# Asking for the first three expert-weight pieces one by one, and splitting weight pieces at other places of a tick

## The chip, the cores and the metric

The kernel runs on one core of one Trainium2 chip. The metric is the device time of one execution in microseconds (us). Engines are called as the profile calls them: PE is the matrix engine (PEld its weight loads), DVE the vector engine, ACT the scalar engine, POOL the general engine, SP the engine that here only issues transfers. A row's "PEclk" is the granted share of PE's full clock of 2.4 GHz; 0.50 is its lower level, 1.2 GHz.

## The reference

Two stages. The first is a delta-rule linear attention over 768 steps for 4 x 8 heads of width 48; the second sends each of the 3072 tokens through one of 8 experts, the one with the largest logit.

```python
k_n = k / (np.linalg.norm(k, axis=-1, keepdims=True) + 1e-06)
for t in range(S):
    kt, vt, bt = (k_n[:, :, t], v[:, :, t], beta[:, :, t, None])
    y[:, :, t] = np.einsum('bhd,bhde->bhe', q[:, :, t], state)
    v_old = np.einsum('bhde,bhd->bhe', state, kt)
    state = state + bt[:, :, :, None] * np.einsum('bhd,bhe->bhde', kt, vt - v_old)
...
expert_idx = np.argmax(x @ w_gate, axis=1)
for e in range(E):
    xe = x[expert_idx == e]
    h = np.maximum(xe @ w1[e], 0.0)
    out[expert_idx == e] = gate_w[expert_idx == e, None] * (h @ w2[e])
```

w1 is 8 x 384 x 1024 and w2 is 8 x 1024 x 384, all in 32-bit floats.

## The kernel before

**The attention part** treats 24 blocks of 128 steps (6 time blocks of each of 4 batches), four at a time, each a quarter further along. The loop over `t` from 0 to 26 makes one *tick* of each step. A tick is a chain over three engines: PE makes `ks` from the state and earlier results (`residual`, L423 and L435), DVE subtracts it from `v_all` (L442), PE applies the block's inverse (`apply`, L450), ACT copies the four results into `u` (L454), PE uses them to finish one block (`finish`: `yp` in L473, the state's update `ku` in L482, `yp` again in L491), then `pq` (L265) for a later block, and then the next tick's `ks`. `xp` (L515) turns a finished block into rows of tokens, between `ks` and `apply`. DVE adds `ku` to the state (L486).

**Routing** runs beside the ticks. `emit_slots` takes two finished blocks, finds each token's expert and slot in small DVE steps (L533 to L581, with the matmuls `pp` in L551 and L554 between `oh_all` and `pos`), and POOL scatters the rows into `xg` in DRAM, one scatter (L588) for each block. After the second scatter of one certain pair SP loads 256 rows of expert 0 back as `xr` (`load_main`, L730); `early` (L783) transposes them in tick 23 and starts expert 0 in the ticks after that.

**Expert weights** come in pieces (`pieces`): per expert three pieces of w1, each 128 x 1024 (512 KB), and four of w2, each 128 x 2 x 384 (384 KB). A piece is asked for by `load` (L708, on SP), lands in one of three raw buffers, and is *split*: ACT casts it to the high part (L693), DVE subtracts that from the piece for the low part (L694). `split` serves other tiles with the same two lines too. A split frees the raw buffer, and right behind it the program asks for the piece three further on. The seven pieces that the table `WSL` of pairs (tick, place) takes in ticks 20 to 23 are all of expert 0.

**The order** is written out by hand. `beside(t, i)` is called at seven places i of each tick; place 0 stands right behind `residual` with its subtraction, place 1 ahead of `apply`, places 3 and 4 behind the copies to `u`, place 6 at the tick's end. Each engine, and SP's queue of transfers, does its instructions in that written order: a transfer that has to wait holds every one behind it on SP.

Of the kernel before, what the change touches and what calls it, by code (L numbers as in the profile page):

```python
# [41 lines left out]
def deltanet_moe(ctx, tc, kt_d, qt_d, kn_d, v_d, beta_d, w_gate, w1, w2, out):  # L42
# [102 lines left out]
    TOK0 = (0, 5, 8, 9, 10)  # L145
    PC0 = (0, 2, 5, 7, 8, 10, 11)

    WSL = ((20, 3), (21, 3), (21, 6), (22, 3), (22, 6), (23, 3), (23, 6))
    ES = ((23, 2), (23, 4), (23, 6), (24, 1), (24, 2), (24, 3), (24, 5), (25, 1), (25, 2), (25, 4), (25, 6), (26, 1), (26, 4))
    EF = (4, 8, 9, 10, 12, 13, 14, 15)  # L150
    EO = 'xxxhhhhhhhhytyyo'
# [516 lines left out]
    def run(gen, steps=1):  # L668

        for _ in range(steps):  # L670
            if next(gen, tiles) is tiles:
                return False
        return True
# [18 lines left out]
    def split(hi, lo, src):  # L692
        nc.scalar.copy(out=hi, in_=src)  # L693
        nc.vector.tensor_tensor(out=lo, in0=src, in1=hi.bitcast(F32), op=ALU.subtract)  # L694

    def pieces():

        todo = []
        for e in range(E):
            for nm, src, kk, ff, st in (("w1", w1[e], KD, FF, 1), ("w2", w2[e], KF, DM, 2)):  # L700
                todo += [(e, nm, src.rearrange("(k p) f -> p k f", p=128), kk, ff, st, j) for j in range(0, kk, st)]
        raws = []

        def load(k):
            e, nm, sv, kk, ff, st, j = todo[k]
            raw = wq[0].tile([128, FF], F32, name=f"{nm}r{e}_{j}", tag="wr", bufs=3)
            raws.append(raw[:, 0:st * ff].rearrange("p (k f) -> p k f", k=st))
            nc.sync.dma_start(out=raws[k], in_=sv[:, j:j + st])  # L708

        for k in range(AH):  # L710
            load(k)
        yield
        for k, (e, nm, sv, kk, ff, st, j) in enumerate(todo):
            if j == 0:
                WW[e][nm] = [wq[e % 2].tile([128, kk, ff], F32R, name=f"{nm}{x}{e}", tag=f"{nm}{x}") for x in "hl"]
            hi, lo = WW[e][nm]
            split(hi[:, j:j + st], lo[:, j:j + st], raws[k])
            if k + AH < len(todo):
                load(k + AH)
            yield  # L720
# [254 lines left out]
    def beside(t, i):  # L975
# [8 lines left out]
        for _ in range(STEPS[i] if t < NN - B else 4):  # L984
            if fine and not run(fine[0]):
                fine.pop(0)
        for _ in range(WSL.count((t, i))):
            run(W)
# [4 lines left out]
    for t in range(NN + LAG):  # L993
        if t < NN and t % B == 0 and t > 0:
            while line and line[0].tb <= t // B:
                inverse_step(t)
            if t == NN - B:
                ep_.close()
                wq.append(ep.enter_context(tc.tile_pool(name="wr", bufs=1, side="right")))
                xq_.append(ep.enter_context(tc.tile_pool(name="xq", bufs=1, side="right")))  # L1000
                W = pieces()
                run(W)
# [343 lines left out]
```

## Time and profile before

| what | value |
|---|---|
| median of 3 runs | 526.83 us (522.76 to 527.09) |
| the profiled execution's own time | 525.81 us |
| its span, first to last instruction | 524.1 us |
| PE / DVE / ACT / POOL busy | 461.2 / 339.3 / 268.2 / 143.8 us |
| mean granted clock | 0.947 |

The profiled execution is 1.7 us longer than its span (what lies around the first and last instruction), and 1.0 us under the median. Busy shares are means over a program of two halves: the ticks of the attention part take the first 300 us or so, with all engines in turn; in the experts behind it PE is nearly always busy. Ticks 20 to 23, which the change touches, lie between 223 and 265 us.

### The profile page before, as it was taken

The page shows a single profiled execution, that of the slowest core. Times are in us where ns is not written, and L with a number is a line of the kernel's source. Part 1 is how long each engine was busy: PE and PEld are TensorE (multiplying, and loading weights), DVE is VectorE, ACT ScalarE, POOL GpSimd, SP SyncE. Part 2 cuts the span into 40 slices and gives each one's busy share as a digit, 9 for nine tenths or more (in the row PEclk, how much of TensorE's full clock was granted, in tenths as well). Part 3 has the DMA queues.
Part 4 walks back from the last instruction along what each step waited for, and adds up shares of the span by engine and source line. Part 5 has one row for each costly group of instructions (what it writes and reads, how often), then busy time and mean ns, then how long its engine had stood idle before and what let it go on. Part 6 is the DMA issues. An engine that isn't in the chain of part 4 may idle for free. (4 is left out here: it accounts for less than half of the span.)

```text
span 524.1 us, 17587 instructions
## 1 busy us (share of the span) xinstructions
PE 461.2 (88%) x7212; PEld 424.4 (81%) x7212; DVE 339.3 (65%) x1024; ACT 268.2 (51%) x622; POOL 143.8 (27%) x305
## 2 busy tenths in 40 slices
PE   5764788979988887977889999999999999999995
PEld 3654677767867776866689899999999999999995
DVE  2989999898989988327554386636372737445330
ACT  2442255776866665846634246535364636344320
POOL 7002021465665555442230301020202020110202
PEclk8877789999999988989999989999999999999998
DMA  5887879687578455574442166555373746453001
GB/s 160 191 265 181 277 177 308 180 239 232 115 236 275 141 182 165 174 253 133 142 154 80 63 170 206 178 168 160 120 227 116 209 127 210 142 163 108 33 3 44
DMA packets 66060, 87.88 MB, mean 168 GB/s; under 512 B 26425, under 2 KB 50767, under 8 KB 65968
## 3 DMA queue, kind: packets, MB, share of 16 engines
q1 hardware_dynamic: 62512, 77.01, 50.0%
q0 software_dynamic: 3456, 9.57, 5.0%
q8 instruction: 67, 1.10, 0.9%
q14 instruction: 25, 0.20, 0.1%
HBM read 60.24 MB, written 23.56 MB: 160 GB/s over the span
## 5 line engine op out<-in xcount | busy, mean ns | idle before, releaser
L769 PE MATMUL y<-w2h,hx 128*128 128x384 f32 x352 | 93.9, 341 | 0.4 <-PEq L1142 0.4
L772 POOL DMA_INDIRECT out_dram<-yo,idx x32 | 30.7, 958 | 202.0 <-ACT yo L1115 129.5
L694 DVE TENSOR_TENSOR w2l<-w2r,w2h 128x768 fp32r<-128x768 f32 x32 | 31.2, 978 | 69.8 <-ACT w2h L693 69.7
L383 DVE TENSOR_TENSOR tmp<-lg,lw 128x99 f32<-128x99 f32 (+29 forms) x253 | 69.1, 308 | 3.0
L387 DVE TENSOR_TENSOR lw<-lw,tmp 128x99 f32<-128x99 f32 (+29 forms) x253 | 68.6, 306 | 0.4
L454 ACT COPY u<-ks 32x384 f32<-32x384 f32 x96 | 45.0, 469 | 44.3 <-PE ks L450 41.4
L769 PEld LDWEIGHTS y<-w2h,hx 128*128 128x128 f32 x352 | 64.1, 188 | 0.7 <-issue 0.7
L769 PE MATMUL y<-w2l,hx 128*128 128x384 f32 x176 | 59.4, 337 | 0.0
L758 PE MATMUL h<-xl,w1h 128*128 128x384 f32 (+1 forms) x168 | 57.5, 342 | 0.2 <-DVE xl L694 0.2
L758 PE MATMUL h<-xh,w1h 128*128 128x384 f32 (+1 forms) x168 | 57.5, 342 | 0.0
L758 PE MATMUL h<-xh,w1l 128*128 128x384 f32 (+1 forms) x168 | 57.4, 342 | 0.0
L450 PE MATMUL ks<-v_all,wt 32*32 32x48 f32 x1536 | 26.8, 209 | 29.5 <-DVE v_all L442 25.1
L450 PEld LDWEIGHTS ks<-v_all,wt 32*32 32x32 f32 x1536 | 22.3, 110 | 34.3 <-DVE v_all L442 28.2
L761 ACT ACTIVATE hx<-h 128x448 fp32r<-128x448 f32 (+1 forms) x64 | 32.7, 517 | 31.6 <-PE h L758 28.6
L276 POOL TENSOR_SCALAR_AFFINE_SELECT pm<-pm 128x1024 f32<-128x1024 f32 x24 | 26.7, 1112 | 79.8 <-ACT pm L275 72.4
L423 PE MATMUL ks<-st,kt 128*32 128x96 f32 x768 | 46.8, 261 | 1.0 <-issue 1.0
L762 DVE SCALAR_TENSOR_TENSOR hx<-h,hx 128x448 fp32r<-128x448 f32 (+1 forms) x64 | 36.8, 586 | 15.0 <-ACT hx L761 14.9
L1115 ACT ACTIVATE yo<-y,gt 128x384 f32<-128x384 f32 x21 | 12.2, 582 | 66.5 <-PE y L769 50.7
L248 ACT COPY gg<-pg 128x512 f32<-128x512 f32 x48 | 25.8, 588 | 31.0 <-PE pg L265 31.0
L423 PEld LDWEIGHTS ks<-st,kt 128*32 128x32 f32 x768 | 35.1, 116 | 4.7 <-issue 1.8
L265 PE MATMUL pq<-qt,kt 64*128 64x128 f32 x384 | 31.7, 296 | 4.0 <-issue 2.8
L265 PEld LDWEIGHTS pq<-qt,kt 64*128 64x128 f32 x384 | 26.3, 197 | 9.1 <-issue 4.4
(194 smaller groups left out, 988.2 us busy)
## 6 DMA issues: line engine op xcount, KB each, us to landing
w1r<-in_w_dram SPq DMA_DIRECT2D x24, 512.0 KB
w2r<-in_w_dram SPq DMA_DIRECT2D x32, 384.0 KB
kt<-in_kt_dram SPq DMA_DIRECT2D x24, 256.0 KB
qt<-in_qt_dram SPq DMA_DIRECT2D x24, 256.0 KB
xg<-zrow SPq DMA_DIRECT2D x7, 788.0 KB
kg<-in_kt_dram SPq DMA_DIRECT2D x17, 256.0 KB
xr<-xg SPq DMA_DIRECT2D x7, 591.0 KB
xn<-row SPq DMA_DIRECT2D x10, 394.0 KB
```

The source lines that it names most:

```text
L265: nc.tensor.matmul(pg[a][:, p], lhsT=kt[r, p], rhs=xt[r, p], start=True, stop=True, tile_position=(64 * a, 0), skip_group_check=True)
L383: nc.vector.tensor_tensor(out=x, in0=lg[:, r0:r1, c:c + 1].broadcast_to([128, r1 - r0, b - a]), in1=lw[:, c:c + 1, a:b].broadcast_to([128, ...
L387: nc.vector.tensor_tensor(out=lw[:, r0:r1, a:b], in0=lw[:, r0:r1, a:b], in1=x, op=ALU.add)
L423: nc.tensor.matmul(ks[32 * q:32 * q + 32, 2 * p:2 * p + 2, :], lhsT=kt_t[n % KTL][:, p, 32 * q:32 * q + 32], rhs=st_view(n % B, p), start= ...
L450: nc.tensor.matmul(ks[r, h, :], lhsT=tiles[n // B]["wt"][r, n % B * H + h, :], rhs=vn[r, h, :], start=True, stop=True, tile_position=(32 * ...
L454: nc.scalar.copy(out=uview(n)[r], in_=ks[r])
L694: nc.vector.tensor_tensor(out=lo, in0=src, in1=hi.bitcast(F32), op=ALU.subtract)
L758: nc.tensor.matmul(ps, lhsT=w[:, d, fs], rhs=x_[:, d], start=(n == 0), stop=(n == len(terms) - 1))
L761: nc.scalar.activation(out=hh, in_=ps, func=AF.Relu)
L762: nc.vector.scalar_tensor_tensor(out=hl, in0=ps, scalar=0.0, in1=hh.bitcast(F32), op0=ALU.max, op1=ALU.subtract)
L769: nc.tensor.matmul(ps, lhsT=h(f)[h_], rhs=w2[w][:, f, :], start=(n == 0), stop=(n == len(terms) - 1))
L772: nc.gpsimd.indirect_dma_start(out=out, out_offset=bass.IndirectOffsetOnAxis(ap=idx, axis=0), in_=yo, in_offset=None, bounds_check=N - 1, ...
```

## The change

In `pieces` the `yield` moves into the loop over the first three loads, so that each call asks for one piece. The first stays where it was, at the start of tick 20; the second and third are asked for at places 2 and 5 of that tick. The table then holds nine pairs in place of seven: two for these loads and seven for the same seven splits, which move from (20,3), (21,3), (21,6), (22,3), (22,6), (23,3), (23,6) to (21,1), (21,3), (22,1), (22,3), (23,0), (23,1), (23,3).

```diff
-    WSL = ((20, 3), (21, 3), (21, 6), (22, 3), (22, 6), (23, 3), (23, 6))
+    WSL = ((20, 2), (20, 5), (21, 1), (21, 3), (22, 1), (22, 3), (23, 0), (23, 1), (23, 3))
...
         for k in range(AH):
             load(k)
-        yield
+            yield
         for k, (e, nm, sv, kk, ff, st, j) in enumerate(todo):
```

No instruction is added or taken away. How the order moves is shown at three places, before first and then after.

SP's queue from the first weight piece on, at the start of tick 20 (`w1r_0` to `w1r_2` are expert 0's w1 pieces, `w2r_0` its first w2 piece, `u` a fill with zeros, `xn` a write of token rows, `ku` and `qt` loads for later ticks):

```order
L708 DMA w1r_0_4492<-in_w_dram 128x1024
L708 DMA w1r_1_4494<-in_w_dram 128x1024
L708 DMA w1r_2_4496<-in_w_dram 128x1024
L412 DMA u_4569<-zrow 96x384
L661 DMA xn<-row_2_4203 128x2x394
L200 DMA ku_4633<-in_kn_dram 128x384
L708 DMA w2r_0_4643<-in_w_dram 128x2x384
L195 DMA qt_117<-in_qt_dram 128x512
L412 DMA u_4720<-zrow 96x384
```

```order
L708 DMA w1r_0_4492<-in_w_dram 128x1024
L412 DMA u_4565<-zrow 96x384
L661 DMA xn<-row_2_4203 128x2x394
L708 DMA w1r_1_4618<-in_w_dram 128x1024
L200 DMA ku_4631<-in_kn_dram 128x384
L708 DMA w1r_2_4648<-in_w_dram 128x1024
L195 DMA qt_117<-in_qt_dram 128x512
L412 DMA u_4714<-zrow 96x384
L708 DMA w2r_0_4728<-in_w_dram 128x2x384
```

The second piece now stands behind the zero fill and the row write, the third behind the load of `ku`, and the first w2 piece behind `qt` and the next fill.

DVE at the end of tick 21 and the start of tick 22 (`sli` is the slot list that the scatters need, `v_all<-v_all,ks` the subtraction of tick 22):

```order
L573 TENSOR_REDUCE sl_all<-pos_0_4797 128x2
L581 CAST sli_0_4830<-sl_all 128x2
L694 TENSOR_TENSOR w1l_4640<-w1r_2_4496,w1h_4639 128x1024
L442 TENSOR_TENSOR v_all<-v_all,ks_4837 128x384
L517 TENSOR_REDUCE rl_2_4883<-xp_2_4884 128x8
L406 TENSOR_TENSOR v_all<-v_all,nt_all 128x384
L486 TENSOR_TENSOR st_137<-st_137,ku_3_4944 48x4x48 x2
```

```order
L573 TENSOR_REDUCE sl_all<-pos_0_4797 128x2
L581 CAST sli_0_4830<-sl_all 128x2
L442 TENSOR_TENSOR v_all<-v_all,ks_4833 128x384
L517 TENSOR_REDUCE rl_2_4879<-xp_2_4880 128x8
L406 TENSOR_TENSOR v_all<-v_all,nt_all 128x384
L694 TENSOR_TENSOR w1l_4725<-w1r_2_4648,w1h_4724 128x1024
L486 TENSOR_TENSOR st_137<-st_137,ku_3_4944 48x4x48 x2
```

The split of the third piece has moved from ahead of the subtraction to behind it.

SP's queue in ticks 22 and 23, from the load of `w2r_4` or what stands ahead of it (`xr` are expert 0's rows, which wait for the scatters; the last row is expert 1's first piece):

```order
L708 DMA w2r_4_4835<-in_w_dram 128x2x384
L412 DMA u_4892<-zrow 96x384
L730 DMA xr_4897<-xg 128x2x394
L708 DMA w2r_6_4960<-in_w_dram 128x2x384
L708 DMA w1r_0_4988<-in_w_dram 128x1024
```

```order
L412 DMA u_4888<-zrow 96x384
L730 DMA xr_4893<-xg 128x2x394
L708 DMA w2r_4_4897<-in_w_dram 128x2x384
L708 DMA w2r_6_4960<-in_w_dram 128x2x384
L708 DMA w1r_0_5030<-in_w_dram 128x1024
```

The piece `w2r_4` was asked for ahead of `xr` and now is behind it.

ACT at the start of tick 23 (`u<-ks` are the copies that PE waits for):

```order
L516 COPY row_2_4882<-xp_3_5032 128x384
L539 COPY row_2_4882<-ids_88 128x2x2
L454 COPY u_4373<-ks_4990 32x384
L454 COPY u_4569<-ks_4990 32x384
L454 COPY u_4720<-ks_4990 32x384
L693 CAST xe<-xt_5096 128x256
L454 COPY u_4892<-ks_4990 32x384
L693 CAST w2h_4956<-w2r_4_4835 128x768
```

```order
L516 COPY row_2_4878<-xp_3_5032 128x384
L539 COPY row_2_4878<-ids_88 128x2x2
L693 CAST w2h_4956<-w2r_4_4897 128x768
L454 COPY u_4373<-ks_4986 32x384
L454 COPY u_4565<-ks_4986 32x384
L454 COPY u_4714<-ks_4986 32x384
L693 CAST xe<-xt_5100 128x256
L454 COPY u_4888<-ks_4986 32x384
```

The cast of `w2r_4` has moved from behind the four copies to ahead of them. On DVE its subtraction now stands ahead of `oh_all` of tick 23, and the first piece's ahead of `oh_all` of tick 21.

## Rows read from the trace of the kernel before

**Rows 1.** The page, DMA queues: packets, MB, share of 16 engines

```profile
q8 instruction: 67, 1.10, 0.9%
```

**Rows 2.** Windows: stretch, length, busy us (count) of each engine, PEclk, DMA share, GB/s

```profile
222.30:227.05 4.75, 4.75 (x130) 3.98 (x129) 1.84 (x5) 3.61 (x9) 3.54 (x11) 1.00 0.93 277
227.05:229.85 2.80, 0.05 (x3) 0.05 (x2) 1.23 (x1) 0.50 (x2) 1.90 (x1) 0.99 1.00 363
229.85:233.65 3.80, 3.80 (x87) 3.43 (x87) 0.00 (x0) 1.07 (x2) 0.00 (x0) 0.56 0.88 280
...
245.60:251.10 5.50, 5.50 (x128) 4.69 (x128) 2.16 (x5) 3.34 (x7) 1.84 (x2) 0.69 0.49 138
...
265.30:300.00 34.70, 33.25 (x427) 30.14 (x427) 14.63 (x72) 12.49 (x31) 5.84 (x6) 1.00 0.25 86
```

**Rows 3.** Timeline of PE, ticks 19 to 24: start, us, what, [idle before <-releaser]

```profile
219.27 1.16 PE L265 MATMUL pq<-qt,kt 64*128 64x128 f32 x16
...
223.18 0.88 PE L450 MATMUL ks<-v_all,wt 32*32 32x48 f32 x64
...
226.12 0.93 PE L265 MATMUL pq<-qt,kt 64*128 64x128 f32 x10
229.81 1.22 PE L265 MATMUL pq<-qt,kt 64*128 64x128 f32 x6 [2.75 <-issue]
...
234.72 0.56 PE L450 MATMUL ks<-v_all,wt 32*32 32x48 f32 x33
236.74 0.54 PE L450 MATMUL ks<-v_all,wt 32*32 32x48 f32 x31 [1.46 <-issue]
...
245.59 0.88 PE L450 MATMUL ks<-v_all,wt 32*32 32x48 f32 x64 [2.05 <-DVE v_all L442]
...
254.92 0.88 PE L450 MATMUL ks<-v_all,wt 32*32 32x48 f32 x64 [1.00 <-DVE v_all L442]
...
257.22 0.17 PE L551 MATMUL pp<-oh_all,ltri 128*128 128x16 bf16 x1 [0.28 <-DVE oh_all L547]
...
265.28 0.88 PE L450 MATMUL ks<-v_all,wt 32*32 32x48 f32 x48 [0.47 <-DVE v_all L442]
```

**Rows 4.** Timeline of DVE at the turn from tick 21 to tick 22

```profile
243.84 1.23 DVE L694 TENSOR_TENSOR w1l<-w1r,w1h 128x1024 fp32r<-128x1024 f32 x1
244.98 0.55 DVE L442 TENSOR_TENSOR v_all<-v_all,ks 128x384 f32<-128x384 f32 x1
...
258.84 0.96 DVE L694 TENSOR_TENSOR w2l<-w2r,w2h 128x768 fp32r<-128x768 f32 x1 [0.67 <-ACT w2h L693]
```

**Rows 5.** Timeline of ACT in ticks 20 to 22

```profile
224.13 1.95 ACT L454 COPY u<-ks 32x384 f32<-32x384 f32 x4 [0.36 <-PE ks L450]
225.98 1.04 ACT L693 CAST w1h<-w1r 128x1024 fp32r<-128x1024 f32 x1
...
252.19 0.85 ACT L693 CAST w2h<-w2r 128x768 fp32r<-128x768 f32 x1
```

**Rows 6.** Timeline of SP: transfers asked for in tick 20, and the load of `xr`

```profile
220.97 1.33 SPq L708 DMA_DIRECT2D w1r<-in_w_dram  x3
222.41 0.52 SPq L412 DMA_DIRECT2D u<-zrow  x1
...
225.36 0.33 SPq L200 DMA_DIRECT2D ku<-in_kn_dram  x1
...
252.83 0.37 SPq L730 DMA_DIRECT2D xr<-xg  x1
```

**Rows 7.** Timeline of POOL: the two scatters ahead of that load

```profile
244.21 1.72 POOL L588 DMA_INDIRECT xg<-row,sli  x1 [1.13 <-DVE sli L581]
249.59 1.52 POOL L588 DMA_INDIRECT xg<-row,sli  x1 [3.66 <-DMA xg<-row,sli]
```

**Rows 8.** Windows right behind that load, columns as in Rows 2

```profile
252.80:253.80 1.00, 1.00 (x9) 0.94 (x8) 0.73 (x1) 0.24 (x1) 0.67 (x1) 1.00 0.08 16
253.80:257.40 3.60, 2.19 (x89) 1.62 (x88) 3.10 (x10) 2.03 (x6) 0.00 (x0) 1.00 0.84 244
```

## The prediction

> **What bounds the kernel now.** I read the page first: PE is busy 88% of the span, but that is a mean over two halves. The windows say where it is not. From 265 to 300 us it is busy 33.25 of 34.70 us [rows 2], so there only less work helps, and this change takes none away; what it can give must come from ticks 20 to 23. PE's timeline shows them [rows 3]. From `pq` at 219.27 to the next `pq` at 226.12 PE waits for nothing, so a tick without a wait takes 6.85 us: 2.94 from `apply` (223.18) to `pq`, 3.91 from `pq` to the next `apply`. Counted from `apply` to `apply`, ticks 20 to 23 take 11.54, 10.87, 9.33 and 10.36 us (starts at 223.18, 234.72, 245.59, 254.92 and 265.28 [rows 3]).
>
> Tick 20: PE stops within `pq` for 2.75 us and "issue" is named: no semaphore, no engine. Behind it the granted clock is 0.56 for 3.8 us, partly the level of 1.2 GHz [rows 2], and from 229.81 to `apply` PE needs 4.91 us where 3.91 - 0.93 = 2.98 would do: 1.93 lost. 6.85 + 2.75 + 1.93 is the 11.5 us. Tick 21: 1.46 us of "issue" in mid-`apply`, then 2.05 us for DVE. Tick 22: 1.00 for DVE, and a clock of 0.69 over 5.5 us [rows 2], which leaves 9.33 - 6.85 - 1.00 = 1.48 for the lower clock. Tick 23 holds early expert work, and 0.47 for DVE.
>
> What is an "issue" pause? The program itself comes by DMA: 67 packets, 1.10 MB, so 16 KB each [rows 1]. From the first pause to the second PE does 6 `pq`, 80 `ks` and 8 `xp` matmuls and 33 of `apply` [rows 3], with the 80 and 8 counted in the code: 127, a regular block. The first comes when three pieces (1,536 KB) were asked for in 1.33 us [rows 6]; DMA then moves 277 GB/s, and 363 in the pause itself, all engines taken [rows 2]. I read it as a page of program that stands in line behind weights. The Trainium skill (Runtime: NRT & Kernel Launch, section Instruction fetch mechanics) says that 16 KiB blocks of 256 instructions are fetched while the one before runs, and that a crossing is mostly hidden; by that the 2.75 us would have another cause, and the loads' spreading would save nothing there. The trace has 2.75 and 1.46 us not hidden, so I go by the trace and keep the other reading as a rival.
>
> **The change part by part.** The same transfers, casts and subtractions are made, so only places count.
>
> *The loads, tick 20.* SP issues in order, and the second piece stands behind a zero fill (144 KB) and a row write (394 KB), neither of which waits long: the fill goes out at 222.41, right behind the pieces [rows 6]. So the place (20,2) in the table does not set its time; it goes out perhaps 1.7 us after the first. The third stands behind `ku`, which goes at 225.36. Ahead of the page then are 512 + 144 + 394 = 1,050 KB, 486 KB fewer, 1.4 to 1.8 us at 363 to 277 GB/s; or 656 KB if the page overtakes the row write, 2.5 to 3.2 us. The pause becomes 0 to 1.35 us; if the second piece gets ahead of the page too, it stays 2.75. I take 0.5, between the first two, since the three pieces went in one run and the page asked for at a fixed point now meets one. After the 1.46 us pause no lower clock cost is seen (236.74 to 245.59 is 8.85, less 2.05 is 6.80, against about 6.35 for what was left of that tick), so the 1.93 goes. Tick 20: 7.35 us, `apply` at 230.5 instead of 234.7.
>
> *What is late next: the page in `apply`.* It stands behind all that was asked for in tick 20. That sum falls by only the first w2 piece (384 KB, 0.39 MB, 1.4 us at 280 GB/s), which now waits for the split at (21,1). So PE goes on not at 236.74 but at 235.3, or 234.6 if one scatter (128 rows, 197 KB, 0.7 us) also falls behind the page; ends 233.5 and 236.0. I take 234.6. PE is there at 230.5 + 0.5 = 231.0 and pauses 3.6 us, over twice as long as before. A pause that long brings back the lower clock: 1.48 to 1.93 us by the two cases above, I take 1.6.
>
> *The splits, tick 21.* The cast at (21,1) (1.04 us) and its subtraction (1.23) fit into that pause, ahead of `oh_all`, and cost nothing; without the pause they would put the copies to `u` and `pp` 0.6 to 1.2 us later. The third piece's subtraction was the last thing on DVE ahead of tick 22's (243.84, 1.23 us, then 244.98 [rows 4]); it leaves, and with the first piece's gone from behind the cast chain the 2.05 us wait goes too (at worst 0.8 stays). `apply` of tick 22: 234.6 + 6.8 + 1.6 = 243.0, 2.6 us earlier than before.
>
> *Tick 22.* No wait for DVE, no lower clock, but the cast at (22,1) is ahead of the copies. They began 0.95 us after `apply` in tick 20 (224.13 [rows 5]); the row copy ends about 0.55 after it, the cast 1.04 later, at 1.6: 0.65 lost. 7.5 us, `apply` of tick 23 at 250.5, 4.4 earlier.
>
> *Tick 23: a new wait.* `w2r_4` is now asked for behind `xr`, and its cast stands ahead of the copies to `u`. `xr` waits for both scatters. Before, the first began at 244.21 and the second 5.4 later, and `xr` went out at 252.83, 3.24 behind the second [rows 6, 7]: 8.6 in all, or 6.5 if the first were as quick as the second; I take 7.2, as less traffic is ahead of the first. The first began 1.4 ahead of an `apply` that was late; I take 0.9 (0.4 to 1.4), so 242.1, and `xr` at 249.3. In the first microsecond behind `xr` almost nothing moved (share 0.08), then 244 GB/s [rows 8]: `xr` and a w2 piece are 0.80 MB, 3.3 us, so the piece is there at 253.6 (4.3 behind; ends 3.9 and 4.5). ACT would cast it 0.75 after `apply` (row copy, a small copy), at 251.25: 2.35 us of waiting, with the copies to `u` behind it on ACT. On DVE `oh_all` stands behind the piece's subtraction, and PE's `pp` behind that: cast 0.85 [rows 5], subtraction 0.96 [rows 4], 0.2 for `oh_all`, so `pp` at 255.6. Before it came 2.30 behind `apply` [rows 3], now that is 252.8: 2.8 us of PE, and 1.5 for the clock behind such a pause, less the 0.47 for DVE. Tick 23: 10.36 + 2.8 + 1.5 - 0.47 = 14.2, and tick 24's `apply` at 264.7 instead of 265.28. Ends: 11.1 if everything is early, 16.7 if late.
>
> *The sum.* 4.2 gained in tick 20, 1.6 given back in 21, 1.8 gained in 22, 3.8 given back in 23: 0.6 us. Behind 265 us PE is the bound and the gain is kept. The profiled execution took 525.81, so **525.2 us**; that execution is 1.0 under the median of 526.83, so a median may lie a microsecond higher.
>
> **The rivals.** *The second page is not late (faster).* If it comes as PE reaches it (231.0), tick 22's `apply` is at 238.5 with the casts' 0.7, tick 23's at 246.0, tick 24's 14.2 later at 260.2: 5.1 less, 520.7. For it: in most ticks no such pause is seen. Against it: in tick 21 one was, behind the same traffic. With `w2r_4` in time as well (11.1) 517.6.
>
> *The pause is not from the loads (no change).* By the rule cited above, the 2.75 stays. Then tick 21's `apply` is at 234.7 as before; its own tick is 6.85 + 0.5 + 1.46 = 8.8, tick 22 7.5, tick 23 14.2: 265.2, and 525.7. Against it: the full DMA engines and the regular block.
>
> *The copies wait longer behind `w2r_4` (slower).* With both scatters as slow as before, tick 23 takes 16.7 us, and tick 24's `apply` is at 267.2: 527.7. It decides from the point at which the piece lands later than about 254.2, 3.7 us behind tick 23's `apply`. For it: the order leaves no other way, and `xr` moves with the ticks, so earlier ticks do not help. Against it: 3.24 us is what a scatter needs with little beside it. Its tail is worse: expert 1's three pieces then follow close on each other, and one more page behind 1,536 KB would cost another 2.75 + 1.93.
>
> **How the numbers follow.** The forecast 0.50; the second page on time 0.22 (0.06 of it with `w2r_4` in time); no effect of the loads 0.10; slower 0.18. The likeliest gives 525.2. The range takes in the faster rival at 520.7 with a microsecond for the unknown first pause, and the slower one with 1.8 for part of its tail: 519.5 to 529.5. A change of 1% is 5.3 us, about what a measurement of this kernel can tell from none (its three runs lie 4.3 apart). Below 520.5 I put 0.18, from the faster rival and early ends; above 531.1 0.10, the slower one's tail; 0.72 between.
>
> **What would show it.** Right: no "issue" pause over 1.4 us in tick 20's `pq`, a longer one in tick 21's `apply` with a low clock behind it, no wait for DVE ahead of tick 22's `apply`, and ACT idle ahead of the cast of `w2r_4` with `xr` asked for shortly before. Wrong: a 2.75 us pause at the same matmul; tick 21 without a pause; or that cast without idle time ahead of it.

## The result and the profile after

The change makes the kernel a little slower: 527.83 us median of 20 runs (523.93 to 533.49), against 525.51 (521.08 to 530.75) of the kernel before measured beside it, ratio 1.0079 with a 95% interval of 1.0050 to 1.0109. Two more measurements (below) gave 1.0047 [1.0006, 1.0087] and 1.0064 [1.0014, 1.0114]. By these ratios 0.5 to 0.8% is lost, 2.5 to 4.2 us; the medians of the three pairs lie 2.3, 1.8 and 2.0 us apart. Ratios and their intervals compare undisturbed runs alone (within 1.5% of their kernel's fastest), medians all runs, and the profiles of e2, e7 and e12 below are of disturbed runs, so no reading rests on them. The forecast was 0.6 us gained; the time itself lies in the stated range.

The profiled execution took 528.31 us, with a span of 526.6 us, 2.5 more than before, and a mean granted clock of 0.939 where it was 0.947. Of the 2.5, 1.42 lie ahead of tick 20 (its `apply` starts at 224.60, before at 223.18). They are there already when the first weight piece goes out (at 222.43, before at 220.97 [rows 6]), and up to that request both programs do the same in the same order; in other profiles that start falls anywhere from 222.4 to 230.3, so it is no effect of the change. From tick 24's `apply` to the end of the span it is 258.8 us in both. The ticks between hold the rest:

| tick | before [rows 3] | forecast | after |
|---|---|---|---|
| 20 | 11.54 | 7.35 | 7.07 |
| 21 | 10.87 | 12.5 | 12.26 |
| 22 | 9.33 | 7.5 | 8.12 |
| 23 | 10.36 | 14.2 | 15.77 |
| sum | 42.10 | 41.55 | 43.22 |

PE's timeline of the changed kernel, with the same columns and lines as [rows 3]:

```profile
224.60 0.88 PE L450 MATMUL ks<-v_all,wt 32*32 32x48 f32 x64
...
227.55 1.48 PE L265 MATMUL pq<-qt,kt 64*128 64x128 f32 x16
...
231.67 0.56 PE L450 MATMUL ks<-v_all,wt 32*32 32x48 f32 x33
234.55 0.86 PE L450 MATMUL ks<-v_all,wt 32*32 32x48 f32 x31 [2.31 <-issue]
...
243.93 0.88 PE L450 MATMUL ks<-v_all,wt 32*32 32x48 f32 x64
...
246.18 0.66 PE L473 MATMUL yp<-qt,st 64*64 64x128 f32 x13 [1.01 <-issue]
...
252.05 0.88 PE L450 MATMUL ks<-v_all,wt 32*32 32x48 f32 x64
...
255.10 0.41 PE L783 MATMUL xt<-ident,xr 128*128 128x128 f32 x2 [1.57 <-DMA xr<-xg]
257.99 0.17 PE L551 MATMUL pp<-oh_all,ltri 128*128 128x16 bf16 x1 [2.48 <-DVE oh_all L547]
...
267.82 0.88 PE L450 MATMUL ks<-v_all,wt 32*32 32x48 f32 x48
```

In tick 20 `pq` is one row of 16 (227.55): the 2.75 us pause is gone. In tick 21 `apply` stops behind its 33rd matmul as before, now for 2.31 us. Tick 22's `apply` (243.93) waits for nothing, but in `yp` behind it (246.18) there is a pause that [rows 3] don't have. In tick 23 PE waits for `xr` and then 2.48 us for `oh_all`. Windows of the same execution, columns as in [rows 2]:

```profile
227.50:231.65 4.15, 4.15 (x107) 3.73 (x104) 0.57 (x2) 1.72 (x5) 1.29 (x2) 1.00 1.02 366
231.65:234.50 2.85, 0.59 (x34) 0.43 (x33) 2.05 (x7) 1.52 (x3) 0.00 (x0) 0.91 0.30 102
234.50:241.20 6.70, 6.65 (x99) 5.61 (x99) 3.63 (x13) 3.57 (x7) 2.08 (x2) 0.53 0.36 102
...
252.00:255.10 3.10, 1.53 (x82) 1.20 (x81) 2.55 (x8) 0.57 (x2) 0.00 (x0) 1.00 1.01 333
255.10:258.00 2.90, 0.42 (x3) 0.25 (x4) 1.04 (x2) 1.90 (x4) 0.00 (x0) 0.98 0.50 200
258.00:264.00 6.00, 6.00 (x46) 4.70 (x48) 2.73 (x10) 3.94 (x10) 0.00 (x0) 0.50 0.62 172
264.00:267.80 3.80, 3.80 (x89) 3.62 (x83) 1.95 (x5) 0.70 (x2) 2.08 (x2) 0.90 0.45 169
267.80:300.00 32.20, 30.63 (x408) 27.80 (x408) 14.23 (x71) 12.29 (x31) 4.86 (x5) 1.00 0.21 71
```

With the loads one by one the DMA engines stay full (share 1.02, 366 GB/s), and the clock at its full level. Behind the pause of tick 21 the granted clock is 0.53 for 6.7 us, behind the wait in tick 23 it is 0.50, the lower level of 1.2 GHz throughout, for 6.0: together over 12 us at or near the lower level, where before it was 0.56 for 3.8 us and 0.69 for 5.5 [rows 2].

ACT and then DVE in tick 23:

```profile
252.53 0.20 ACT L539 COPY row<-ids 128x4 f32<-128x4 f32 x1
256.03 0.83 ACT L693 CAST w2h<-w2r 128x768 fp32r<-128x768 f32 x1 [3.30 <-DMA w2r<-in_w_dram]
256.88 1.46 ACT L454 COPY u<-ks 32x384 f32<-32x384 f32 x3
```

```profile
243.02 0.56 DVE L442 TENSOR_TENSOR v_all<-v_all,ks 128x384 f32<-128x384 f32 x1 [1.87 <-PE ks L435]
...
254.68 0.17 DVE L544 TENSOR_REDUCE m<-oh 128x2 f32<-128x16 f32 x1
256.89 0.96 DVE L694 TENSOR_TENSOR w2l<-w2r,w2h 128x768 fp32r<-128x768 f32 x1 [2.04 <-ACT w2h L693]
257.77 0.17 DVE L547 TENSOR_TENSOR oh_all<-oh,m 128x16 bf16<-128x16 f32 x1
```

ACT stands idle for 3.30 us for a w2 piece, ahead of the copies to `u`; on DVE the piece's subtraction stands ahead of `oh_all`, and PE gets `pp` at 257.99, 5.94 us behind `apply`, where it was 2.30 [rows 3]. The first DVE row is tick 22's subtraction, which now waits for `ks` alone: the third piece's split is behind it. What SP had asked for, and POOL's scatters ahead of it (compare [rows 6, 7]):

```profile
250.24 0.37 SPq L730 DMA_DIRECT2D xr<-xg  x1
250.70 0.93 SPq L708 DMA_DIRECT2D w2r<-in_w_dram  x2
252.59 0.34 SPq L708 DMA_DIRECT2D w1r<-in_w_dram  x1
```

```profile
243.70 0.99 POOL L588 DMA_INDIRECT xg<-row,sli  x1 [0.16 <-DVE v_all L442]
246.58 1.03 POOL L588 DMA_INDIRECT xg<-row,sli  x1 [1.89 <-DMA xg<-row,sli]
```

The second scatter starts 2.88 us behind the first (before 5.4), and `xr` goes out at 250.24, 6.54 us behind the first scatter. `w2r_4` is cast 5.8 us after that. The second w2 piece and expert 1's first w1 piece were asked for right behind it, and share the DMA engines (share 1.01): from 250.20 to the cast some 1.5 MB move (windows of 67, 333 and 413 GB/s), where `xr` and one w2 piece are 0.80.

### The profile page after: what moved, and what is told of

Its sections match the earlier page's. It is cut to its first block, busy times and chain, and to the rows that moved or that the text cites. A ratio compares the mean times of both kernels' runs of the same rounds, so it can differ in the third digit from the quotient of the medians.

```text
span 526.6 us, 17587 instructions
## 1 busy us (share of the span) xinstructions
PE 464.5 (88%) x7212; PEld 427.1 (81%) x7212; DVE 336.1 (64%) x1024; ACT 269.2 (51%) x622; POOL 146.6 (28%) x305
## 5 line engine op out<-in xcount | busy, mean ns | idle before, releaser
L387 DVE TENSOR_TENSOR lw<-lw,tmp 128x99 f32<-128x99 f32 (+29 forms) x253 | 70.6, 314 | 0.4
L383 DVE TENSOR_TENSOR tmp<-lg,lw 128x99 f32<-128x99 f32 (+29 forms) x253 | 67.4, 301 | 3.0
L276 POOL TENSOR_SCALAR_AFFINE_SELECT pm<-pm 128x1024 f32<-128x1024 f32 x24 | 30.7, 1281 | 85.6 <-ACT pm L275 82.9
L450 PE MATMUL ks<-v_all,wt 32*32 32x48 f32 x1536 | 25.6, 206 | 26.2 <-DVE v_all L442 21.4
L265 PE MATMUL pq<-qt,kt 64*128 64x128 f32 x384 | 33.0, 309 | 0.7 <-ACT gg L248 0.7
L769 PEld LDWEIGHTS y<-w2l,hx 128*128 128x128 f32 x176 | 33.2, 188 | 0.0
```

The lines of the kernel that those rows point to most:

```text
L265: nc.tensor.matmul(pg[a][:, p], lhsT=kt[r, p], rhs=xt[r, p], start=True, stop=True, tile_position=(64 * a, 0), skip_group_check=True)
L276: nc.gpsimd.affine_select(out=pm, in_=pm, compare_op=ALU.is_gt, fill=0.0, base=0, pattern=[[0, H], [1, C]], channel_multiplier=-1)
L383: nc.vector.tensor_tensor(out=x, in0=lg[:, r0:r1, c:c + 1].broadcast_to([128, r1 - r0, b - a]), in1=lw[:, c:c + 1, a:b].broadcast_to([128, ...
L387: nc.vector.tensor_tensor(out=lw[:, r0:r1, a:b], in0=lw[:, r0:r1, a:b], in1=x, op=ALU.add)
L450: nc.tensor.matmul(ks[r, h, :], lhsT=tiles[n // B]["wt"][r, n % B * H + h, :], rhs=vn[r, h, :], start=True, stop=True, tile_position=(32 * ...
L769: nc.tensor.matmul(ps, lhsT=h(f)[h_], rhs=w2[w][:, f, :], start=(n == 0), stop=(n == len(terms) - 1))
```

## The experiments

The theory after the result: spreading the loads helps or is neutral; the loss is `w2r_4` behind `xr`, its cast and subtraction ahead of the copies and of `oh_all`, and the lower clock behind that wait and behind the pause in `apply`. Rivals: the loads themselves do harm; casts ahead of the copies do harm wherever `w2r_4` stands; the pauses just vary. Ratios are to the kernel before on the same chip, with 95% intervals; "ticks" is the stretch from tick 20's to tick 24's `apply` in the one profiled execution.

### The loads alone, and the splits alone

e1 and e9 (the same kernel again): loads spread, splits where they were. The loads are not quite those of the change: the third piece is asked for right behind the second, ahead of the load of `ku`, and in the change behind it.

```diff
-    WSL = ((20, 2), (20, 5), (21, 1), (21, 3), (22, 1), (22, 3), (23, 0), (23, 1), (23, 3))
+    WSL = ((20, 1), (20, 2), (20, 3), (21, 3), (21, 6), (22, 3), (22, 6), (23, 3), (23, 6))
```

> Half of the change: the three loads one by one (second and third behind the zero fill and the row write, ahead of ku), splits at the old places, w2r_4 ahead of xr and its cast behind the copies. Theory T (the loss is the new wait for w2r_4 in tick 23 with the lower clock behind it): the 2.75 us pause in pq goes, a pause in tick 21's apply stays (1.5 to 3), tick 23 keeps some 10.4 us, no wait of ACT for w2r_4; 2 to 4 us faster than before, ratio 0.992 to 0.997. Rival R (the loads themselves do the harm, by moving a program page behind other transfers): slower than before, ratio 1.003 to 1.010.

> The loads spread over tick 20, splits at the places of the kernel before, once more beside the two kernels with the new splits. Theory (spreading the loads takes the pause out of tick 20 and costs nothing elsewhere): ratio 0.987 to 0.995, ticks 20 to 23 together 37 to 39 us, no issue pause over 1.1 us in tick 20's pq. Rival (the first measurement of this kernel, 6 undisturbed runs, was luck): ratio 0.997 to 1.003.

e2 and e10: loads at once, splits where the change has them.

```diff
-            yield
+        yield
...
-    WSL = ((20, 2), (20, 5), (21, 1), (21, 3), (22, 1), (22, 3), (23, 0), (23, 1), (23, 3))
+    WSL = ((21, 1), (21, 3), (22, 1), (22, 3), (23, 0), (23, 1), (23, 3))
```

> The other half: three loads at once as before, the seven splits at the new places. T: the 2.75 us pause in tick 20 stays, no wait for DVE ahead of tick 22's apply, tick 23 takes 14 to 16 us with PE waiting for oh_all and xr; 2 to 5 us slower than before, ratio 1.004 to 1.010. R: within 1 us of before or faster, ratio 0.996 to 1.002.

> The three loads at once, splits at the new places, once more. Theory (the new splits put w2r_4 behind xr and its cast and subtraction ahead of the copies to u and of oh_all): ratio 1.002 to 1.010, PE waits 2 us or more for oh_all in tick 23. Rival (the splits are neutral and the harm comes from the two edits together): ratio 0.996 to 1.001.

Measured: loads alone 0.9893 [0.9840, 0.9947] and 0.9955 [0.9906, 1.0003], ticks 37.33 and 38.60 us. Splits alone 1.0026 [0.9987, 1.0065] and 1.0106 [1.0046, 1.0166], ticks 41.28 in e10. On either chip the splits alone are slower than the loads alone, with intervals that don't touch. So loads spread in this order do no harm, and the new splits carry a loss. The change's own loads, with the third behind `ku`, were not run with the old splits; what that place costs is taken up below. e10 also holds a surprise: with three loads at once its tick 20 took 7.46 us, with no pause in `pq` and one of 0.31 us in `ks`.

### Taking out the wait of tick 23

e3, e11 and e15 (three measurements of one kernel): the change, but `xr` is asked for right behind `w2r_4`.

```diff
-            load_main(0, 0, G0)
+            held.append(0)
...
+        if held and (t, i) >= (22, 1):
+            load_main(held.pop(), 0, G0)
```

> The changed kernel, but xr is asked for right behind w2r_4 in place of ahead of it. T: ACT's wait of 3.3 us for w2r_4 goes, PE's wait of 2.5 us for oh_all goes, its wait for xr (1.6) stays, the lower clock behind is shorter or gone; tick 23 takes 11 to 12.5 us in place of 15.8; 3 to 4.5 us faster than the changed kernel, ratio to the kernel before 0.998 to 1.002. R2 (what costs is that casts stand ahead of the copies at all, and the pauses for program pages): under 1 us faster than the changed kernel, ratio 1.006 to 1.010.

> The change with one thing undone: xr is asked for right behind w2r_4 and no longer ahead of it; beside the change itself on one chip. Theory (the loss is w2r_4's wait behind xr and the lower clock behind it): 4 to 6 us faster than the change's own run, ratio to the kernel before 0.990 to 0.997, no wait of PE for oh_all over 1 us in tick 23 and the clock at its full level there. Rival (casts ahead of the copies are the loss wherever w2r_4 stands): within 2 us of the change, ratio 1.002 to 1.008.

> The change with xr asked for behind w2r_4, a third measurement, to decide between 0.9938 and 1.0088. Theory: tick 23 of 11 to 12 us, ratio 0.992 to 1.000. Rival: tick 23 as short, but ratio 1.002 to 1.009, so that tick 23's gain is lost where the profile of one execution does not show it.

e4: the change, with the splits of `w2r_4` and `w2r_6` at (23,3) and (23,6), behind the copies; `w2r_4` stays behind `xr`.

```diff
-    WSL = ((20, 2), (20, 5), (21, 1), (21, 3), (22, 1), (22, 3), (23, 0), (23, 1), (23, 3))
+    WSL = ((20, 2), (20, 5), (21, 1), (21, 3), (22, 1), (22, 3), (23, 0), (23, 3), (23, 6))
```

> The changed kernel, but the casts of w2r_4 and w2r_6 stand behind the copies of tick 23 (places 3 and 6, as before); w2r_4 is still asked for behind xr. T: ACT still waits for w2r_4, but with nothing of PE's behind it but yt, and oh_all does not wait; tick 23 takes 11 to 13 us; 2 to 4.5 us faster than the changed kernel, ratio 0.998 to 1.004. R2: as e3, within 1 us of the changed kernel.

e14: the change with the third split at (21,6), one place earlier, so that `w2r_4` is again asked for ahead of `xr`.

```diff
-    WSL = ((20, 2), (20, 5), (21, 1), (21, 3), (22, 1), (22, 3), (23, 0), (23, 1), (23, 3))
+    WSL = ((20, 2), (20, 5), (21, 1), (21, 3), (21, 6), (22, 3), (23, 0), (23, 1), (23, 3))
```

> The change, but the third split at (21,6) and no longer at (22,1), so that w2r_4 is asked for ahead of xr; its cast stays ahead of the copies to u. Theory: no wait of ACT for w2r_4 in tick 23 and none of PE for oh_all over 1.2 us, tick 23 of 11 to 12 us, a wait of 1 to 2 us for DVE ahead of tick 22's apply in its place; ratio to the kernel before 0.991 to 0.999. Rival (the loss is not tick 23's wait): ratio 1.003 to 1.008.

e13 goes the other way: it puts only that wait into the kernel with the loads alone.

```diff
-    WSL = ((20, 1), (20, 2), (20, 3), (21, 3), (21, 6), (22, 3), (22, 6), (23, 3), (23, 6))
+    WSL = ((20, 1), (20, 2), (20, 3), (21, 3), (22, 1), (22, 3), (22, 6), (23, 1), (23, 3))
```

> The loads spread over tick 20 and the splits of the kernel before, but the third split at (22,1), and those of w2r_4 and w2r_6 at (23,1) and (23,3), as in the change: so w2r_4 is asked for behind xr, and its cast and subtraction stand ahead of the copies to u and of oh_all. Theory (that wait is the change's loss): tick 23 of 14 us or more, PE waiting 2 us or more for oh_all, ticks 20 to 23 together 41 to 45 us, ratio to the kernel before 1.000 to 1.006, some 3 to 6 us above the kernel with the loads alone (0.9893 and 0.9955). Rival (tick 23's wait costs a profile but not the median): ratio 0.989 to 0.996.

ACT in tick 23 of e13, then PE there, then the windows:

```profile
251.68 0.83 ACT L693 CAST w2h<-w2r 128x768 fp32r<-128x768 f32 x1 [3.58 <-DMA w2r<-in_w_dram]
252.53 1.46 ACT L454 COPY u<-ks 32x384 f32<-32x384 f32 x3
```

```profile
248.48 0.88 PE L450 MATMUL ks<-v_all,wt 32*32 32x48 f32 x64 [0.99 <-DVE v_all L442]
...
250.74 0.41 PE L783 MATMUL xt<-ident,xr 128*128 128x128 f32 x2 [0.78 <-DMA xr<-xg]
253.64 0.17 PE L551 MATMUL pp<-oh_all,ltri 128*128 128x16 bf16 x1 [2.49 <-DVE oh_all L547]
```

```profile
248.48:254.00 5.52, 2.25 (x88) 1.80 (x88) 2.88 (x9) 2.24 (x4) 0.00 (x0) 0.84 0.79 269
254.00:260.50 6.50, 6.50 (x57) 5.19 (x59) 3.16 (x11) 3.82 (x9) 0.83 (x1) 0.50 0.64 225
```

The same in e3: ACT, and the windows of ticks 20, 21 and 23:

```profile
252.23 0.83 ACT L693 CAST w2h<-w2r 128x768 fp32r<-128x768 f32 x1
253.09 1.46 ACT L454 COPY u<-ks 32x384 f32<-32x384 f32 x3
```

```profile
226.94:234.53 7.59, 7.24 (x217) 6.19 (x217) 1.91 (x5) 4.08 (x9) 4.05 (x12) 1.00 0.96 337
234.53:244.27 9.74, 7.36 (x221) 6.23 (x220) 7.12 (x22) 6.76 (x14) 3.40 (x4) 1.00 0.46 129
251.66:263.35 11.69, 8.91 (x212) 7.42 (x211) 8.15 (x25) 6.92 (x16) 2.07 (x2) 1.00 0.78 243
```

In e13 ACT waits 3.58 us for the piece, PE 2.49 for `oh_all`, and 6.5 us at 0.50 follow; in e3 the cast of `w2r_4` has no wait, the copies begin 1.43 us behind `apply`, and the clock stays at its full level. And in e4, where `w2r_4` is behind `xr` but the copies don't stand behind its cast, PE loses 1.21 us:

```profile
255.14 0.88 PE L450 MATMUL ks<-v_all,wt 32*32 32x48 f32 x64
...
258.20 0.17 PE L551 MATMUL pp<-oh_all,ltri 128*128 128x16 bf16 x1 [1.21 <-DVE oh_all L547]
```

Tick 23 in all other profiles, in us, by the two things that the change moved there:

| | cast ahead of the copies | cast behind them |
|---|---|---|
| `w2r_4` behind `xr` | after 15.77, e10 14.68, e13 16.20, e5 15.66 | e4 10.80 |
| `w2r_4` ahead of `xr` | e3 11.69, e11 11.00, e15 11.46, e14 11.07 | before 10.36 and 11.19, e1 11.10, e9 11.23, e6 11.29, e16 10.64 |

The last cell has a mean of 10.97 us. Casts ahead of the copies alone stand 0.0 to 0.7 us above it, both together 3.7 to 5.2. So in tick 23 it is not the casts wherever the piece stands, but the two together. The cell of e4 alone weighs little: its tick 22 took 10.54 us, and `w2r_4` went out 3.11 us ahead of tick 23's `apply` (252.03 and 255.14) where it was 1.35 in the change, so that the piece was less late there.

The ratios show less of it. e3, e11 and e15 gave 0.9938 [0.9874, 1.0002], 1.0088 [1.0009, 1.0167] and 0.9974 [0.9930, 1.0018], which don't agree; e14 gave 1.0043 [1.0003, 1.0083], e4 1.0016 [0.9955, 1.0077], e13 0.9990 [0.9930, 1.0050]. So e13 stands above the two measurements of the loads alone by 0.35 to 0.97%, 1.8 to 5.1 us, where 3 to 6 was expected, with intervals that touch; e14, whose ticks took 37.41 us in its profile, is no faster than the kernel before. In the ratio e15 came out as its theory had it, e14 as its rival, e11 above its rival's range, and e13 between theory and rival; on e11's chip the change itself, e12, has 1.0064 beside e11's 1.0088. A part of the reason is that a profile shows one execution: e14's profiled one was the fastest of its 12 (524.10 of 524.10 to 532.65 us).

The granted clock, which every execution records, goes with the ratios. Among the executions that they compare, e14's mean clock is 0.948 beside 0.955 of the kernel before, e11's 0.949 beside 0.958, e10's 0.934 beside 0.958, the change's 0.946 beside 0.952 and 0.946 beside 0.958; e1's, with the best ratio, 0.954 beside 0.956. Over the 14 kernels with a ratio, the ratio falls as the kernel's own clock rises beside that of the kernel before (correlation -0.81), and 0.006 of a 526 us span are 3.2 us of PE's time. The lower clock needn't stand in these ticks. One window of e14, then the same of e6, some 23 to 48 us behind tick 24's `apply`:

```profile
285.00:310.00 25.00, 24.25 (x190) 22.56 (x189) 13.87 (x59) 9.57 (x23) 4.72 (x10) 0.86 0.35 113
```

```profile
285.00:310.00 25.00, 23.27 (x201) 21.25 (x200) 14.57 (x62) 10.18 (x24) 4.72 (x10) 1.00 0.36 113
```

The same work is done, at a clock of 0.86 in one and 1.00 in the other; PE is busy 24.25 and 23.27 us.

### The pages of the program

In the view of DMA queues a narrow window shows when the program's own 16 KB packets pass. For the changed kernel, the quarter microsecond from 232.00, and for the kernel before the one from 227.25, inside its 2.75 us pause:

```profile
q8 instruction: 1, 0.02, 23.9%
```

```profile
DMA packets 27, 0.12 MB, mean 492 GB/s; under 512 B 0, under 2 KB 0, under 8 KB 26
...
q8 instruction: 1, 0.02, 23.9%
```

PE goes on at 234.55 and 229.81, some 2.5 us after each. In twelve other pauses, of the kernel before and of e1, e3, e4, e5, e8, e13 and e15, it is 2.3 to 2.8 us from the start of the packet's quarter microsecond too (before, tick 21: 234.25 and 236.74; e13: 228.75 and 231.10; e3: 233.75 and 236.57). So the "issue" pauses are pages, as the prediction took them. The Trainium skill (Runtime: NRT & Kernel Launch, section Instruction fetch mechanics) calls the crossing of such a block mostly hidden. The trace agrees in part: of seven packets between 219 and 253.5 us of the kernel before five end in no pause of over a microsecond, but two do, of 2.75 and 1.46 us.

e5: the change, with the third load at place (21,0), so behind `qt`.

```diff
-    WSL = ((20, 2), (20, 5), (21, 1), (21, 3), (22, 1), (22, 3), (23, 0), (23, 1), (23, 3))
+    WSL = ((20, 2), (21, 0), (21, 1), (21, 3), (22, 1), (22, 3), (23, 0), (23, 1), (23, 3))
```

> The change, but the third load one place later, behind tick 21's first casts' place (21,0), so behind qt on SP. Theory (the pause in tick 21's apply is a page of the program that stands in line behind the loads): 2.31 us becomes 1.5 or less, since 512 KB fewer are ahead of it, and the stretch at the lower clock behind it goes; tick 21 takes 8.5 to 10.5 us in place of 12.26, unless the third piece's split now waits for it. Rival (pause not from the loads): 2.0 to 2.6 us stay.

SP's request for it, and PE's pause:

```profile
232.15 0.42 SPq L708 DMA_DIRECT2D w1r<-in_w_dram  x1
```

```profile
236.63 0.56 PE L450 MATMUL ks<-v_all,wt 32*32 32x48 f32 x33
239.78 0.54 PE L450 MATMUL ks<-v_all,wt 32*32 32x48 f32 x31 [2.59 <-issue]
```

A miss: the pause is 2.59 us, what the rival expected, and tick 21 13.42. The expectation was ill drawn. The request is only 1.1 us later behind `apply` than in the change (3.69 against 2.57 us), and the page's packet, in the quarter microsecond from 237.25, still passes 5.1 us behind it (4.8 in the change, 4.2 to 4.5 in e3 and e4). That the page moved with the load does not show a line behind it: PE too came to tick 21's `apply` 1.1 us later (tick 20 took 8.17 us, in the change 7.07).

The other profiles say more. SP in the changed kernel, then in e1 (`ku` and the last of the three w1 pieces):

```profile
226.79 0.33 SPq L200 DMA_DIRECT2D ku<-in_kn_dram  x1
227.17 0.49 SPq L708 DMA_DIRECT2D w1r<-in_w_dram  x1
```

```profile
228.26 2.06 SPq L708 DMA_DIRECT2D w1r<-in_w_dram  x2
230.99 0.41 SPq L200 DMA_DIRECT2D ku<-in_kn_dram  x1
```

In the seven profiles with the third piece behind `ku` (the change, e3, e4, e5, e11, e14, e15) the pause in tick 21's `apply` is 1.30 to 2.59 us (to 2.31 without e5, which was run only once, at 533.69 us), and a stretch at the lower clock follows within that tick in five. In the five with it ahead of `ku` (e1, e6, e9, e13, e16) the pause is 0 to 1.17 us, and such a stretch follows in one. Tick 20 takes 7.59 us in the mean of either group, so PE is no later in one than in the other. The first split differs between the groups too, but at (20,3), as in the second, it asks for the next piece sooner and not later. So the place of the third load most likely costs something of its own, by a page in line behind it, as the prediction took it; the change with only that load moved ahead of `ku` was not run.

### How much varies by itself, and a mixture

e7 and e12: the change once more; e8: the kernel before once more, for a second profile.

> The changed kernel once more, beside the kernel before on the same chip. Theory: slower again by some 1 to 4 us (ratio 1.002 to 1.008), ticks 20 to 23 together 42.5 to 44.5 us with a wait of 2 us or more of PE for oh_all in tick 23 and a stretch at the lower clock behind it. Rival (the pauses that a profile shows differ from run to run as much as the kernels do): ticks 20 to 23 differ from 43.2 by over 2 us, and the ratio's interval holds 1.

> The changed kernel as it is, for the comparison with the three others of this chip: ratio to the kernel before 1.002 to 1.009; ticks 20 to 23 together 43 to 47 us, tick 23 alone 15 us or more with PE waiting 2 us or more for oh_all.

> The kernel before once more, for a second profile: ticks 20 to 23 within 1.5 us of the 42.1 of the first (pauses at the same matmuls) if the pauses belong to the program's order; 2 us or more off if they differ from run to run. The start of tick 20's apply anywhere from 222 to 229.5 us.

PE's pauses in e8:

```profile
224.51 0.88 PE L450 MATMUL ks<-v_all,wt 32*32 32x48 f32 x64
...
229.42 0.71 PE L265 MATMUL pq<-qt,kt 64*128 64x128 f32 x6 [1.04 <-issue]
...
234.29 0.54 PE L450 MATMUL ks<-v_all,wt 32*32 32x48 f32 x31 [0.94 <-issue]
```

Same program, same two places, but 1.04 and 0.94 us in place of 2.75 and 1.46 [rows 3]; ticks 20 to 23 take 8.27, 11.57, 9.42 and 11.19, together 40.45 against 42.10, 1.65 us off, between the two bounds of the expectation. In these two profiles the places are the same and the lengths belong to the execution.

e6 and e16: loads spread, every split at place 0 or 3, behind the copies, `xr` behind `w2r_4`.

```diff
-    WSL = ((20, 2), (20, 5), (21, 1), (21, 3), (22, 1), (22, 3), (23, 0), (23, 1), (23, 3))
+    WSL = ((20, 1), (20, 2), (20, 3), (21, 3), (22, 0), (22, 3), (23, 0), (23, 3), (24, 0))
...
-            load_main(0, 0, G0)
+            held.append(0)
...
+        if held and (t, i) >= (22, 0):
+            load_main(held.pop(), 0, G0)
```

> The loads spread over tick 20, xr asked for ahead of w2r_4 no longer (w2r_4 first, then xr), and each split at place 0 or 3, so that casts stand behind the copies to u and the third subtraction behind tick 22's own. Theory (the loss of the change sits in tick 23: w2r_4 behind xr with its cast ahead of the copies, and the lower clock behind that wait; the loads themselves help): no pause over 1.4 us in tick 20's pq, no wait for DVE over 0.5 us ahead of tick 22's apply, none of ACT for w2r_4, PE's wait for xr of 1 to 2 us stays; ticks 20 to 23 together 35 to 37 us, against 42.1 before and 43.2 for the change; ratio to the kernel before 0.986 to 0.99. Rival (splits behind the copies make other work late, as in the kernel before): a wait for DVE or ACT of 1 us or more at some tick and 38 us or more together, ratio 0.99 to 0.995. If the whole difference between kernels lies elsewhere than in these ticks: ratio 0.997 to 1.003.

> All splits behind the copies, loads spread, xr behind w2r_4, once more: ratio 0.991 to 0.998 if the first 0.9946 holds, 0.999 to 1.003 if it was luck.

Measured: 0.9946 [0.9907, 0.9984] and 0.9996 [0.9958, 1.0034], ticks 36.84 and 35.64 us, among the shortest (e3 has 36.41). By its expectation the second measurement says that the first was luck. Beside e7, the change on its chip, e6 is 1.0% faster, with intervals that don't touch. No kernel here beats the one before by a sure 1%; the loads alone (e1, e9) come nearest, and are the smaller edit.

All runs together settle more than the single ratios. Take the times of all 314 runs of these kernels and of the kernel before beside them, give each chip a level of its own, and fit three terms by least squares: spread loads give 2.0 us (standard error 0.5), the third load behind `ku` costs 1.7 (0.6), and `w2r_4` behind `xr` with its cast ahead of the copies costs 2.5 (0.5). From the executions that the ratios compare it is 1.9, 2.1 and 3.3. For the change the three add up to a loss of 2.2 or 3.5 us, which is what was measured. Casts ahead of the copies stand mostly in the kernels with the third load behind `ku`; given a term of their own, they get 0.9 (0.9), the third load 1.2 (0.8) and the wait 1.9 (0.7), so these two can't be told apart for sure.

## Why the prediction was wrong, by its own steps

**What bounds the kernel**: right. The time behind tick 24's `apply` didn't change between the two profiles, and the ticks decided. The pause is a page of program: right, by its packets.

**Tick 20** (7.35): 7.07, with no pause where 0.5 was taken. But "4.2 gained" rests on the 11.54 us of one execution. e8 has 8.27 with the three loads at once, e10 7.46; twelve profiles with the loads spread have 7.07 to 8.17. The gain is 0 to 4.2 us by the execution, and 2.8 by the mean of the two profiles of the kernel before (9.9): the second term of the sum that was mis-sized.

**Tick 21** (12.5): 12.26, by two errors that cancel. PE went on at 234.55, and that this meets the forecast 234.6 is luck, since the whole program ran 1.42 us later: PE was there at 232.23 and not at 231.0, and paused 2.31 us and not 3.6. The lower clock behind it cost not 1.6: 6.7 us at 0.53 is 3.15 us of lost clock. 6.85 + 2.31 + 3.15 = 12.3.

**Tick 22** (7.5): 8.12. The wait for DVE is gone, as forecast. The 1.01 us pause for a page in `yp` was not foreseen; e4 and e10 have it too (1.18 and 1.16), e6 1.50.

**Tick 23** (14.2): 15.77. This is the step that failed first, by its size: the mechanism was forecast as it came, at the place, on the engines and in the order named. `xr` went out 6.54 us behind the first scatter (7.2 taken), but "4.3 behind" for `w2r_4` was 5.8: [rows 8] were read for `xr` and one piece, and the two pieces asked for right behind shared the engines. So `pp` came 5.94 us behind `apply` and not 5.1: 3.64 lost in place of 2.8. And the clock: "1.5" was some 2.2, what is left of the 5.4 with the 3.64 taken off and the 0.47 for DVE put back; the granted clock would allow 3.4 (6.0 us at 0.50 and 3.8 at 0.90). 5.4 us were given back where 3.8 was taken.

**The sum**: 42.10 to 43.22 in place of 41.55, 1.67 us too low, of which tick 23 is 1.57, tick 22 0.62, and ticks 20 and 21 together -0.52. Measured by both profiles of the kernel before (42.10 and 40.45, mean 41.28), 1.9 us are lost where 0.6 gained was forecast: of the 2.5 between, 1.4 is tick 20's gain, taken from one execution, and 1.2 tick 23; ticks 21 and 22 cancel. The medians have 1.8 to 2.3 lost, which leaves nothing to explain; the ratios have 2.5 to 4.2. If they are nearer, the rest goes with more of the lower clock in executions that no profile shows; in which of their stretches stays open.

**The rivals.** The slower one came about. That its 527.7 meets the median of 527.83 is luck: its ticks sum to 44.0 and were 43.22, and the profiled 528.31 holds 1.42 from ahead of the ticks. Its point was a piece that lands later than 3.7 us behind tick 23's `apply`, and the cast began 3.98 behind it. Its reason was another: the scatters were quick, and the transfers slow. The page that is not late did not come in the changed kernel (2.31 us), nor in e3, e4, e11, e14 and e15 with the same order up to there (1.30 to 2.31). It did come, with 0 to 0.75 us, in e6, e9, e13 and e16, where the third piece is ahead of `ku`. That the pause is not from the loads is not borne out for tick 20: six of twelve profiles with loads spread have no pause there, six have 0.35 to 0.93 us; with loads at once it is 2.75, 1.04 and, in e10, none. It falls less clearly than it would without e10.

## What to carry to other kernels

Where one queue serves a load that waits and a load that doesn't, look who stands in front: a piece whose request slips behind a waiting one, and whose consumer stands ahead of the critical copies on its engine, cost 3.7 to 5.2 us of a tick, and some 2.5 us of the whole by all runs together; the consumer ahead of the copies with the piece in time cost that tick under one. Price a long stop of PE with the lower clock behind it, here 2 to 3 us beside 2.3 to 3.6 us of stop, and read the mean granted clock of all runs, not of one profile. And before a gain is taken from a pause in one execution, read a second one: the same pause was 2.75 and 1.04 us.

## What the hardware showed that I had not expected

- The lower clock behind a stop lasted 3.8 us at 0.56 behind 2.75 us [rows 2], 6.7 at 0.53 behind 2.31, 6.0 at 0.50 behind the waits for `xr` and `oh_all`, 10.2 at 0.50 in e13 (252.30 to 262.50); in e3 none behind 1.48. The length of the stop does not tell it.
- A page of the program needs some 2.5 us from its packet to PE's next matmul, also where DMA is nearly idle (share 0.30 in the changed kernel's pause).
- The same instructions up to tick 20 end anywhere from 222.4 (e13) to 230.3 us (e10), one profile each, an 8 us spread that is larger than what the change costs.
